# Another order and other PSUM banks ahead of the first MLP layer, and the first quarter of w_in in two loads

## The chip, the core and the metric

The kernel runs on one core of a Trainium2 chip. The metric is the device time of one execution in microseconds (us). Before the change the median of three runs is 305.06 us (304.82 to 306.04).

## What is computed

The reference is a sparse attention followed by a two-layer MLP. The attention has 8 batches of 8 heads, 576 positions and a head size of 64. Heads 0 to 3 look at the last 32 positions ("local"), heads 4 to 7 at all earlier positions with the same remainder mod 32 ("strided").

In short, with the softmax written as one function:

```python
scores = scale * np.matmul(q, k.transpose(0, 1, 3, 2))
mask_local = (rel >= 0) & (rel < stride)
mask_strided = (rel >= 0) & (pos[None, :] % stride == pos[:, None] % stride)
masks = np.stack([mask_local if h < H // 2 else mask_strided for h in range(H)], axis=0)
attn = softmax(np.where(masks, scores, -1e9))
x = (attn @ v).transpose(0, 2, 1, 3).reshape(4608, 512)
h = x @ w_in                                  # 512 -> 2048
g = np.where(h > 0.0, h, np.exp(np.minimum(h, 0.0)) - 1.0)
out = g @ w_out                               # 2048 -> 512
```

## The kernel before, in words

**Tiling.** The 4608 tokens go through the MLP in 9 chunks of 512. `xT` holds the attention output transposed: 128 partitions, 4 column blocks c, all tokens. Blocks c = 0 and 1 come from the local heads, c = 2 and 3 from the strided heads. `w_in` comes in four loads of 512 of its 2048 columns; each of its 16 column tiles m (128 wide) gives one PSUM tile h of layer 1, in four matmuls, one for each c. ELU is an Exp on ScalarE, a clamp and a max on VectorE, which writes `g`; layer 2 takes `g` and `w_out`.

The attention of a batch has four pairs of heads: `0s0` is batch 0, strided, first pair; `0s1` the second strided pair; `0l0` and `0l1` the local pairs. In batches 0 and 1 pair y of a kind fills one whole block of xT: `0l0` c = 0, `0l1` c = 1, `0s0` c = 2, `0s1` c = 3. Each pair is worked on in two halves u = 0 and 1.

**What sets the order.** The kernel runs under a manual schedule: `ORDER` (lines 35 to 145) is a list of tokens, and lines 702 to 704 issue them in that order. Each engine runs its own instructions strictly in that order; waits between engines follow from the data, from PSUM banks and from buffer pools. The eight PSUM banks are named in the tokens by hand. A matmul that writes a bank waits until whoever read that bank last is done. A token is a letter, then its arguments:

- `w.7.512.512`: filler matmuls on zeros (line 389), here two of 512 columns into bank 7; nobody reads them.
- `T.0s1.q.7`: transposes of q of pair 0s1 on TensorE into bank 7 (lines 403, 409, 412). The pair 0s0 goes in halves, from f32 data staged early. `c` copies a transpose out of PSUM on VectorE, `C` on ScalarE (lines 422 to 430).
- `S.0l1.1.23`: the scores of half u = 1 into banks 2 and 3 (line 455). `e`: Exp on ScalarE (462). `m`: the mask product on VectorE (469 strided, 475 local).
- `O.0l1.1.41`: the product with v, into bank 4, and the row sums, a product with ones, into bank 1 (482, 491 strided; 498, 503 local; function `pv`). `n`: Ln of the sums on ScalarE (553). `r`: Exp of minus that (558). `x`: the product on VectorE that writes xT (583).
- `V.0`: a VectorE copy of 32 rows of local v (587), which the local products with v need.
- `a.0.15.1`: layer 1 of chunk 0, tile m = 15, blocks c = 2 and 3, into bank 1. `b.0.15`: the same tile, blocks c = 0 and 1. `L`: all four blocks (function `l1`, line 610). `h`: the Exp of ELU (618). `i`, `j`: the clamp on VectorE or ScalarE; `g`: the max (636, 638). `Z`: layer 2 (644).
- `D`: a load, issued by GpSimd (POOL) (lines 233 to 280). `D.wi3.0` is the quarter of w_in with tiles 12 to 15; wi0, wi2 and wi1 follow. With one more argument, which no token of this ORDER uses, the quarter comes in two parts: .0 is the blocks c = 2 and 3, .1 the blocks 0 and 1 (lines 273 to 276). `F.mk` makes the local mask on POOL (348, 351) and `F.ml` lays it out on VectorE (356, 358).

Buffers that matter here: `e` has two, so the third Exp waits for the mask product of the first; `ln` has three, so an `n` waits for the `x` three before it; POOL has eight semaphores for loads, so a load is issued once the load eight before it has landed.

The stage that the change touches is all that stands ahead of layer 1: the attention of batch 0, some 22 us. Behind it the list of tokens stays as it is.

Of the kernel before, what the change touches and what calls it, by code (L numbers as in the profile page):

```python
# [33 lines left out]

ORDER = """
w.7.512.512.512.512.512.512.512.512 F.v1 D.kl.0.1 D.vs.0.0 F.vp D.ql.0.1 F.ms D.vs.0.1 T.0s0.q.0.7
D.kl.0.0 T.0s0.k.0.6 c.0s0.q.0 D.ql.0.0 c.0s0.k.0 w.0.512.512.172 T.0s0.k.1.7 S.0s0.0.01 C.0s0.k.1
T.0s0.q.1.6 e.0s0.0 D.vl.0 c.0s0.q.1 w.2.512.512.512 T.0s1.q.7 T.0s1.k.6 D.wi3.0 c.0s1.q S.0s0.1.01
C.0s1.k m.0s0.0 T.0l1.k.5 D.wi0.0 e.0s0.1 c.0l1.k w.2.403 S.0s1.1.67 S.0s1.0.23 e.0s1.1 m.0s0.1
w.4.512.406 T.0l1.q.5 e.0s1.0 m.0s1.1 D.wi2.0 O.0s0.1.47 c.0l1.q O.0s1.1.61 n.0s0.1 m.0s1.0 D.wi1.0  # L40
S.0l1.1.23 n.0s1.1 e.0l1.1 w.0.370 T.0l0.k.7 D.qs.1 O.0s0.0.51 r.0s1.1 O.0s1.0.03 F.mk r.0s0.1 T.0l0.q.2
x.0s1.1 C.0l0.k x.0s0.1 D.wo0.0 c.0l0.q n.0s1.0 w.5.224.224.224.224.206 S.0l1.0.67 n.0s0.0 F.ml
S.0l0.1.23 e.0l1.0 D.ks.1 r.0s1.0 w.4.512.512 S.0l0.0.67 m.0l1.1 r.0s0.0 m.0l1.0 x.0s1.0 e.0l0.0
w.4.512.512 V.0 e.0l0.1 O.0l1.1.41 x.0s0.0 n.0l1.1 O.0l1.0.07 m.0l0.0 D.wo1.0 n.0l1.0 O.0l0.0.32 m.0l0.1
r.0l1.1 O.0l0.1.75 r.0l1.0 x.0l1.1 x.0l1.0 n.0l0.0 a.0.15.1 n.0l0.1 a.0.14.6 r.0l0.0 a.0.12.4 r.0l0.1
a.0.13.5 D.wo2.0 x.0l0.0 x.0l0.1 D.wo3.0 b.0.15 b.0.14 h.0.15 b.0.12 h.0.14 i.0.15 b.0.13 a.0.0.0 h.0.12
b.0.0 a.0.1.2 b.0.1 i.0.14 g.0.15 h.0.0 a.0.3.7 D.vs.1 a.0.11.3 j.0.12 g.0.14 a.0.2.1 h.0.1 i.0.0 b.0.2
g.0.12 b.0.3 h.0.2 g.0.0 b.0.11 h.0.3 a.0.8.6 i.0.2 D.ql.1 h.0.11 i.0.1 a.0.6.4 g.0.2 h.0.13 a.0.5.0
b.0.8 g.0.1 a.0.4.1 D.kl.1 h.0.8 i.0.3 b.0.4 g.0.3 b.0.5 h.0.4 T.1s1.q.2 a.0.7.7 j.0.13 i.0.4 b.0.6
C.1s1.q g.0.4 b.0.7 D.vl.1 h.0.5 g.0.13 Z.0.1.0.2 h.0.6 i.0.5 Z.0.0.0.5 g.0.5 h.0.7 D.qs.2 j.0.6 i.0.8  # L50
a.0.9.1 i.0.7 a.0.10.0 g.0.8 b.0.9 g.0.6 j.0.11 b.0.10 g.0.7 h.0.9 T.1s1.k.6 Z.0.3.0.4 D.ks.2 h.0.10
g.0.11 j.0.10 Z.0.3.1.4 i.0.9 c.1s1.k g.0.10 Z.0.0.1.5 g.0.9 Z.0.1.1.2 D.kl.2 T.1s0.q.3 T.1s0.k.7
C.1s0.q Z.0.1.2.2 c.1s0.k S.1s0.1.01 S.1s1.0.67 Z.0.0.2.5 e.1s1.0 e.1s0.1 Z.0.0.3.5 m.1s0.1 m.1s1.0
S.1s1.1.01 S.1s0.0.67 e.1s1.1 Z.0.1.3.2 e.1s0.0 m.1s1.1 O.1s0.1.31 o.0.1 m.1s0.0 O.1s1.0.07 T.1l1.q.6
n.1s0.1 n.1s1.0 Z.0.3.2.4 c.1l1.q r.1s0.1 q.0.0 D.vs.2 r.1s1.0 O.1s1.1.76 x.1s1.0 T.1l1.k.5 n.1s1.1
O.1s0.0.21 c.1l1.k T.1l0.q.0 n.1s0.0 T.1l0.k.6 x.1s0.1 D.ql.2 Z.0.3.3.4 C.1l0.k c.1l0.q r.1s1.1 V.1
S.1l0.1.01 r.1s0.0 S.1l0.0.56 x.1s1.1 Z.0.2.0.3 e.1l0.0 q.0.3 X.qs.2 e.1l0.1 m.1l0.0 S.1l1.1.56 e.1l1.1
m.1l0.1 S.1l1.0.01 O.1l0.0.74 e.1l1.0 X.ks.2 m.1l1.1 O.1l0.1.65 x.1s0.0 Z.0.2.1.3 n.1l0.0 n.1l0.1
m.1l1.0 r.1l0.0 O.1l1.1.54 t.0.3 r.1l0.1 x.1l0.0 O.1l1.0.21 n.1l1.1 x.1l0.1 Z.0.2.2.3 n.1l1.0 r.1l1.1
t.0.0 r.1l1.0 Z.0.2.3.3 x.1l1.1 x.1l1.0 X.kl.2 W.2 L.1.12.7 L.1.1.6 h.1.12 i.1.12 L.1.6.5 h.1.1 g.1.12  # L60
o.0.2 D.qs.3 L.1.0.4 i.1.1 h.1.6 g.1.1 L.1.4.7 h.1.0 i.1.6 g.1.6 L.1.5.6 X.ql.2 h.1.4 D.ks.3 i.1.0 j.1.4
L.1.3.5 g.1.0 D.vs.3 h.1.5 t.0.1 g.1.4 L.1.2.4 D.vl.2 h.1.3 i.1.5 i.1.3 h.1.2 g.1.3 L.1.10.7 S.2s1.0.01
S.2s1.1.23 e.2s1.0 g.1.5 D.ql.3 e.2s1.1 L.1.15.5 i.1.2 h.1.10 g.1.2 L.1.7.6 h.1.15 m.2s1.1 i.1.15
S.2s0.0.01 S.2s0.1.23 h.1.7 X.qs.3 g.1.15 L.1.13.4 e.2s0.1 i.1.10 j.1.7 L.1.9.5 m.2s0.1 g.1.10 L.1.8.3
g.1.7 h.1.9 e.2s0.0 i.1.9 L.1.14.7 X.ks.3 h.1.13 g.1.9 L.1.11.6 h.1.8 i.1.13 h.1.14 i.1.8 Z.1.2.0.5
# [83 lines left out]
def kernel(  # L149
# [455 lines left out]
    def l1(ch, m, cs, bk=None):  # L605
        ch, m = int(ch), int(m)
        if bk is not None:
            tiles["h", ch, m] = ps[:, int(bk), :]
        for c in cs:
            nc.tensor.matmul(  # L610
                tiles["h", ch, m], lhsT=w_in_sb[:, c, m * 128:(m + 1) * 128],
                rhs=xT[:, c, ch * CHUNK:(ch + 1) * CHUNK],
                start=(c == 2), stop=(c == 1), skip_group_check=True)
# [121 lines left out]
```

## Time and profile before

| | |
|---|---|
| median of three runs | 305.06 us |
| lowest and highest run | 304.82 and 306.04 us |
| the profiled execution's own time | 305.3 us |
| its span, first to last instruction | 303.6 us |
| ScalarE (ACT) busy | 222.9 us (73%) |
| VectorE (DVE) busy | 224.4 us (74%) |
| loads by POOL (queue q0) | 19.47 MB |

The profile has one such execution. PE is the matmul side of TensorE, PEld its weight loads. In a timeline the first column is the start in us, the second the time until the group's last instruction ends; `x8` is how many instructions are in the group, and a bracket says how long the engine sat idle before it and what ended that. Matmuls overlap: the time from one start to the next counts, not their duration. Ends of matmuls are modelled. A table by stretches gives the busy time of each engine in each stretch, with the number of instructions in brackets.

### The profile page before, as it was taken

The page shows a single profiled execution, that of the slowest core. Times are in us where ns is not written, and L with a number is a line of the kernel's source. Part 1 is how long each engine was busy: PE and PEld are TensorE (multiplying, and loading weights), DVE is VectorE, ACT ScalarE, POOL GpSimd, SP SyncE. Part 2 cuts the span into 40 slices and gives each one's busy share as a digit, 9 for nine tenths or more (in the row PEclk, how much of TensorE's full clock was granted, in tenths as well). Part 3 has the DMA queues.
Part 4 walks back from the last instruction along what each step waited for, and adds up shares of the span by engine and source line. Part 5 has one row for each costly group of instructions (what it writes and reads, how often), then busy time and mean ns, then how long its engine had stood idle before and what let it go on. Part 6 is the DMA issues. An engine that isn't in the chain of part 4 may idle for free.

```text
span 303.6 us, 6241 instructions
## 1 busy us (share of the span) xinstructions
PE 297.1 (98%) x2331; PEld 147.5 (49%) x2331; DVE 224.4 (74%) x440; ACT 222.9 (73%) x402; POOL 81.5 (27%) x111
## 2 busy tenths in 40 slices
...
GB/s 165 187 206 206 207 194 166 168 223 146 128 143 152 191 193 138 160 143 164 140 188 208 73 173 163 129 38 36 38 69 0 37 35 0 37 36 0 37 138 104
DMA packets 107357, 37.62 MB, mean 124 GB/s; under 512 B 89152, under 2 KB 102848, under 8 KB 107328
## 3 DMA queue, kind: packets, MB, share of 16 engines
q0 software_dynamic: 69728, 19.47, 63.6%
...
## 4 chain that ended last, share of the span: by engine, by line
PE 89%; ACT 5%; DVE 3%; issue 1%; DVEq 0%; ACTq 0%
PE ps L610 38%; PE ps L644 38%; PE ps L455 3%; PE ps L389 2%; PE ps L518 2%; PE ps L525 2%; ACT e L462 1%; ACT ln L558 1%; ACT ln L553 1%; PE ps L674 1%; DVE g L638 1%; DVE he L627 1%; PE ps L412 1%; PE ps L403 1%; PE ps L409 1%
## 5 line engine op out<-in xcount | busy, mean ns | idle before, releaser
L644 PE MATMUL ps<-w_out_sb,g 128*128 128x512 bf16 x560 | 133.4, 379 | 0.0
L610 PE MATMUL ps<-xT,w_in_sb 128*128 128x512 bf16 x576 | 131.2, 379 | 0.8 <-DVE xT L583 0.4
L618 ACT ACTIVATE he<-ps 128x512 f32<-128x512 f32 x144 | 80.2, 596 | 25.8 <-PE ps L610 24.8
L610 PEld LDWEIGHTS <-w_in_sb 128*128 128x128 bf16 x576 | 54.9, 98 | 65.3 <-issue 1.9
L644 PEld LDWEIGHTS <-g 128*128 128x128 bf16 x560 | 50.8, 98 | 54.2
L638 DVE TENSOR_TENSOR g<-he,ps 128x512 bf16<-128x512 bf16 x103 | 68.3, 681 | 1.6
L583 DVE TENSOR_TENSOR xT<-ps,ln 64x576 bf16<-64x576 f32 (+1 forms) x64 | 42.6, 678 | 22.8 <-ACT ln L558 21.2
L627 DVE TENSOR_SCALAR he<-he 128x512 bf16<-128x512 f32 x103 | 44.0, 440 | 12.5 <-ACT he L618 11.8
L462 ACT ACTIVATE e<-ps 72x576 bf16<-72x576 f32 (+1 forms) x64 | 38.7, 647 | 9.9 <-PE ps L455 7.8
L553 ACT ACTIVATE ln<-ps 64x576 f32<-64x576 f32 (+1 forms) x64 | 36.4, 584 | 9.2 <-PE ps L518 5.1
L558 ACT ACTIVATE ln<-ln 64x576 f32<-64x576 f32 (+1 forms) x64 | 38.4, 621 | 1.2
L636 DVE SCALAR_TENSOR_TENSOR g<-he,ps 128x512 bf16<-128x512 bf16 x41 | 27.4, 679 | 4.9 <-ACT he L625 4.7
L625 ACT ACTIVATE he<-he 128x512 bf16<-128x512 f32 x41 | 25.4, 630 | 1.8 <-DVE g L638 1.1
...
L650 ACT COPY osb<-ps 128x512 f32<-128x512 f32 x17 | 9.9, 584 | 17.3 <-PE ps L644 10.6
L650 DVE COPY osb<-ps 128x512 f32<-128x512 f32 x18 | 12.2, 684 | 13.5 <-PE ps L644 13.4
...
L475 DVE TENSOR_TENSOR pm<-e,mask_l 128x576 bf16<-128x576 bf16 x32 | 14.2, 454 | 7.4 <-ACT e L462 6.5
L469 DVE TENSOR_TENSOR pm<-e,mask_s 72x576 bf16<-72x576 bf16 x32 | 14.2, 448 | 3.7 <-ACT e L462 3.3
L233 POOL DMA_DIRECT2D vs<-in_v_dram x8 | 5.3, 658 | 32.0 <-DVE vsp L590 31.0
L233 POOL DMA_DIRECT2D ks<-in_k_dram x7 | 4.8, 685 | 27.6 <-DMA kTs<-ks 25.8
L518 PEld LDWEIGHTS <-vsp 72*128 72x128 bf16 x192 | 9.3, 98 | 5.5 <-DVE pm L469 0.5
...
## 6 DMA issues: line engine op xcount, KB each, us to landing
...
```

The costliest lines, as they stand in the source:

```text
L462: nc.scalar.activation(e[0:R], tiles.pop(("S", key, u))[0:R], ACT.Exp, scale=scale)
L553: nc.scalar.activation(t, s_ps, ACT.Ln)
L558: nc.scalar.activation(t, t, ACT.Exp, scale=-1.0)
L583: nc.vector.tensor_mul(dst, o_ps, rc)
L610: nc.tensor.matmul(tiles["h", ch, m], lhsT=w_in_sb[:, c, m * 128:(m + 1) * 128], rhs=xT[:, c, ch * CHUNK:(ch + 1) * CHUNK], start=(c == 2) ...
L618: nc.scalar.activation(e, tiles["h", i[0], i[1]], ACT.Exp)
L625: nc.scalar.activation(e1, e, ACT.Relu, bias=1.0, scale=-1.0)
L627: eng.tensor_scalar(e1, e, scalar1=1.0, scalar2=1.0, op0=ALU.min, op1=ALU.subtract)
L636: nc.vector.scalar_tensor_tensor(dst, e1, -1.0, h, op0=ALU.mult, op1=ALU.max)
L638: nc.vector.tensor_tensor(dst, e1, h, op=ALU.max)
L644: nc.tensor.matmul(ops, lhsT=g[ch % 2][:, m, kk * 128:(kk + 1) * 128], rhs=w_out_sb[:, m, :], start=(m == 0), stop=(m == MC - 1), skip_gro ...
L650: eng(o_sb, tiles.pop(("o", int(ch), int(kk))))
```

## The change

The tokens ahead of layer 1 stand in another order, with other banks; three new things are in the code.

1. **Fillers.** `w.0` loses one of 512 columns, and `w.2` (three of 512, then one of 403) is gone. Behind them five groups with 4438 columns become four groups, of two or three fillers of 512, with 5120 columns. Seven fewer filler matmuls in all.
2. **Second pair at once.** `T.0s1.q` and `T.0s1.k` follow `T.0s0.q.1` directly, into banks 3 and 4.
3. **Pair 0's products first.** `O.0s0.0` and `O.0s0.1`, with their `n`, `r`, `x`, come ahead of those of 0s1; before, three of the four came the other way round. `m.0s1.0` now stands ahead of `c.0l1.q`, `n.0s1.1` ahead of `e.0l1.1`; all four strided `r` come ahead of `e.0l1.0`; all four strided `x` and `F.ml` come ahead of `m.0l1.0` and `V.0`.
4. **Masks early.** `F.mk` goes from behind `D.qs.1` to behind the first w_in quarter on POOL, and `F.ml` moves up on VectorE.
5. **w_in's first quarter in two loads,** `D.wi3.0.0` (blocks 2 and 3) and `D.wi3.0.1`.
6. **Layer 1.** `a.0.15.1` moves between the products of 0l1 and those of 0l0. Blocks 1 and 0 are taken in that order everywhere (`b`, `L`), and for the tiles 15, 14, 12 of chunk 0 block 1 of all three (`p`) comes ahead of block 0 (`P`).

```diff
-D.kl.0.0 T.0s0.k.0.6 c.0s0.q.0 D.ql.0.0 c.0s0.k.0 w.0.512.512.172 T.0s0.k.1.7 S.0s0.0.01 C.0s0.k.1
-T.0s0.q.1.6 e.0s0.0 D.vl.0 c.0s0.q.1 w.2.512.512.512 T.0s1.q.7 T.0s1.k.6 D.wi3.0 c.0s1.q S.0s0.1.01
-C.0s1.k m.0s0.0 T.0l1.k.5 D.wi0.0 e.0s0.1 c.0l1.k w.2.403 S.0s1.1.67 S.0s1.0.23 e.0s1.1 m.0s0.1
-w.4.512.406 T.0l1.q.5 e.0s1.0 m.0s1.1 D.wi2.0 O.0s0.1.47 c.0l1.q O.0s1.1.61 n.0s0.1 m.0s1.0 D.wi1.0
-S.0l1.1.23 n.0s1.1 e.0l1.1 w.0.370 T.0l0.k.7 D.qs.1 O.0s0.0.51 r.0s1.1 O.0s1.0.03 F.mk r.0s0.1 T.0l0.q.2
-x.0s1.1 C.0l0.k x.0s0.1 D.wo0.0 c.0l0.q n.0s1.0 w.5.224.224.224.224.206 S.0l1.0.67 n.0s0.0 F.ml
-S.0l0.1.23 e.0l1.0 D.ks.1 r.0s1.0 w.4.512.512 S.0l0.0.67 m.0l1.1 r.0s0.0 m.0l1.0 x.0s1.0 e.0l0.0
-w.4.512.512 V.0 e.0l0.1 O.0l1.1.41 x.0s0.0 n.0l1.1 O.0l1.0.07 m.0l0.0 D.wo1.0 n.0l1.0 O.0l0.0.32 m.0l0.1
-r.0l1.1 O.0l0.1.75 r.0l1.0 x.0l1.1 x.0l1.0 n.0l0.0 a.0.15.1 n.0l0.1 a.0.14.6 r.0l0.0 a.0.12.4 r.0l0.1
-a.0.13.5 D.wo2.0 x.0l0.0 x.0l0.1 D.wo3.0 b.0.15 b.0.14 h.0.15 b.0.12 h.0.14 i.0.15 b.0.13 a.0.0.0 h.0.12
+D.kl.0.0 T.0s0.k.0.6 c.0s0.q.0 D.ql.0.0 c.0s0.k.0 w.0.512.172 T.0s0.k.1.7 S.0s0.0.01 C.0s0.k.1
+T.0s0.q.1.6 e.0s0.0 D.vl.0 c.0s0.q.1 T.0s1.q.3 T.0s1.k.4 D.wi3.0.0 c.0s1.q S.0s0.1.01 C.0s1.k m.0s0.0
+T.0l1.k.5 D.wi3.0.1 e.0s0.1 c.0l1.k S.0s1.1.67 S.0s1.0.23 e.0s1.1 m.0s0.1 w.4.512.512 e.0s1.0 m.0s1.1
+F.mk O.0s0.0.40 D.wi0.0 D.wi2.0 O.0s0.1.51 n.0s0.0 T.0l1.q.6 n.0s0.1 m.0s1.0 r.0s0.0 c.0l1.q w.7.512.512
+r.0s0.1 F.ml S.0l1.1.23 O.0s1.1.70 D.wi1.0 x.0s0.0 n.0s1.1 x.0s0.1 O.0s1.0.61 e.0l1.1 T.0l0.k.4 n.0s1.0
+T.0l0.q.5 m.0l1.1 D.qs.1 r.0s1.1 c.0l0.q r.0s1.0 x.0s1.1 C.0l0.k S.0l1.0.01 x.0s1.0 w.2.512.512.512
+e.0l1.0 S.0l0.0.45 S.0l0.1.23 D.wo0.0 m.0l1.0 V.0 e.0l0.0 D.ks.1 m.0l0.0 w.7.512.512.512 e.0l0.1
+O.0l1.1.41 n.0l1.1 O.0l1.0.56 m.0l0.1 a.0.15.1 D.wo1.0 n.0l1.0 O.0l0.0.07 r.0l1.1 O.0l0.1.23 r.0l1.0
+x.0l1.1 x.0l1.0 n.0l0.0 n.0l0.1 a.0.14.6 r.0l0.0 a.0.12.4 r.0l0.1 a.0.13.5 p.0.15 p.0.14 p.0.12 D.wo2.0
+x.0l0.0 x.0l0.1 D.wo3.0 P.0.15 P.0.14 h.0.15 P.0.12 h.0.14 i.0.15 b.0.13 a.0.0.0 h.0.12 b.0.0 a.0.1.2
...
-                start=(c == 2), stop=(c == 1), skip_group_check=True)
+                start=(c == 2), stop=(c == 0), skip_group_check=True)
...
-        "a": lambda ch, m, bk: l1(ch, m, (2, 3), bk), "b": lambda ch, m: l1(ch, m, (0, 1)),
-        "L": lambda ch, m, bk: l1(ch, m, (2, 3, 0, 1), bk), "h": exp_h,
+        "a": lambda ch, m, bk: l1(ch, m, (2, 3), bk), "b": lambda ch, m: l1(ch, m, (1, 0)),
+        "p": lambda ch, m: l1(ch, m, (1,)), "P": lambda ch, m: l1(ch, m, (0,)),
+        "L": lambda ch, m, bk: l1(ch, m, (2, 3, 1, 0), bk), "h": exp_h,
```

The tokens behind `h.0.12` are the same in both kernels.

More of the change, by code (lines that the diff above doesn't have):

```diff
@@ L47 @@
[L47 to L61, printed above, removed]
@@ L62 @@
-L.1.3.5 g.1.0 D.vs.3 h.1.5 t.0.1 g.1.4 L.1.2.4 D.vl.2 h.1.3 i.1.5 i.1.3 h.1.2 g.1.3 L.1.10.7 S.2s1.0.01
+D.kl.0.0 T.0s0.k.0.6 c.0s0.q.0 D.ql.0.0 c.0s0.k.0 w.0.512.172 T.0s0.k.1.7 S.0s0.0.01 C.0s0.k.1
+T.0s0.q.1.6 e.0s0.0 D.vl.0 c.0s0.q.1 T.0s1.q.3 T.0s1.k.4 D.wi3.0.0 c.0s1.q S.0s0.1.01 C.0s1.k m.0s0.0
+T.0l1.k.5 D.wi3.0.1 e.0s0.1 c.0l1.k S.0s1.1.67 S.0s1.0.23 e.0s1.1 m.0s0.1 w.4.512.512 e.0s1.0 m.0s1.1
+F.mk O.0s0.0.40 D.wi0.0 D.wi2.0 O.0s0.1.51 n.0s0.0 T.0l1.q.6 n.0s0.1 m.0s1.0 r.0s0.0 c.0l1.q w.7.512.512
@@ new lines @@
+x.0l0.0 x.0l0.1 D.wo3.0 P.0.15 P.0.14 h.0.15 P.0.12 h.0.14 i.0.15 b.0.13 a.0.0.0 h.0.12 b.0.0 a.0.1.2
+b.0.1 i.0.14 g.0.15 h.0.0 a.0.3.7 D.vs.1 a.0.11.3 j.0.12 g.0.14 a.0.2.1 h.0.1 i.0.0 b.0.2 g.0.12 b.0.3
+h.0.2 g.0.0 b.0.11 h.0.3 a.0.8.6 i.0.2 D.ql.1 h.0.11 i.0.1 a.0.6.4 g.0.2 h.0.13 a.0.5.0 b.0.8 g.0.1
+a.0.4.1 D.kl.1 h.0.8 i.0.3 b.0.4 g.0.3 b.0.5 h.0.4 T.1s1.q.2 a.0.7.7 j.0.13 i.0.4 b.0.6 C.1s1.q g.0.4
+b.0.7 D.vl.1 h.0.5 g.0.13 Z.0.1.0.2 h.0.6 i.0.5 Z.0.0.0.5 g.0.5 h.0.7 D.qs.2 j.0.6 i.0.8 a.0.9.1 i.0.7
@@ new lines @@
+a.0.10.0 g.0.8 b.0.9 g.0.6 j.0.11 b.0.10 g.0.7 h.0.9 T.1s1.k.6 Z.0.3.0.4 D.ks.2 h.0.10 g.0.11 j.0.10
+Z.0.3.1.4 i.0.9 c.1s1.k g.0.10 Z.0.0.1.5 g.0.9 Z.0.1.1.2 D.kl.2 T.1s0.q.3 T.1s0.k.7 C.1s0.q Z.0.1.2.2
+c.1s0.k S.1s0.1.01 S.1s1.0.67 Z.0.0.2.5 e.1s1.0 e.1s0.1 Z.0.0.3.5 m.1s0.1 m.1s1.0 S.1s1.1.01 S.1s0.0.67
+e.1s1.1 Z.0.1.3.2 e.1s0.0 m.1s1.1 O.1s0.1.31 o.0.1 m.1s0.0 O.1s1.0.07 T.1l1.q.6 n.1s0.1 n.1s1.0
+Z.0.3.2.4 c.1l1.q r.1s0.1 q.0.0 D.vs.2 r.1s1.0 O.1s1.1.76 x.1s1.0 T.1l1.k.5 n.1s1.1 O.1s0.0.21 c.1l1.k
```

7 lines of the change are left out of this document (added).

## The prediction

> **What bounds the kernel now.** I read the page's busy times, then the table by stretches, then the chain of waits ahead of layer 1, then each engine's timeline there.
>
> ```profile
> span 303.6 us, 6241 instructions
> PE 297.1 (98%) x2331; PEld 147.5 (49%) x2331; DVE 224.4 (74%) x440; ACT 222.9 (73%) x402; POOL 81.5 (27%) x111
> 22.00:30.00 8.00, 8.00 (x45) 3.78 (x44) 6.54 (x14) 5.64 (x12) 2.08 (x4) 1.00 1.24 206
> 100.00:200.00 100.00, 99.98 (x795) 49.00 (x793) 83.27 (x154) 87.69 (x153) 33.95 (x41) 1.00 1.24 157
> ```
>
> The first two numbers of a stretch row are its length and PE's busy time: behind the 22nd microsecond PE is never let go for long. So the kernel's time is the moment at which layer 1 runs, plus a fixed amount of matmul work. What the change moves lies ahead of that. I therefore ask one thing: when does PE reach `b.0.13`, the first matmul behind the rewritten tokens that is the same in both? What it gains there it should keep to the end.
>
> ```profile
> 15.27 0.61 PE L389 MATMUL ps<-zero 128*128 128x512 bf16 x2
> 15.80 0.31 PE L498 MATMUL ps<-pm,ones 128*64 128x288 bf16 x2
> 16.48 0.23 PE L503 MATMUL ps<-pm,vl 128*64 128x96 bf16 x1 [0.36 <-DVE vl L587]
> 16.88 0.32 PE L503 MATMUL ps<-pm,vl 128*64 128x96 bf16 x5 [0.17 <-issue]
> 16.99 0.32 PE L498 MATMUL ps<-pm,ones 128*64 128x288 bf16 x2
> 17.70 0.31 PE L498 MATMUL ps<-pm,ones 128*64 128x288 bf16 x2
> 18.07 1.90 PE L610 MATMUL ps<-xT,w_in_sb 128*128 128x512 bf16 x8
> 20.33 9.23 PE L610 MATMUL ps<-xT,w_in_sb 128*128 128x512 bf16 x42 [0.35 <-DVE xT L583]
> ```
>
> The row at 20.33 starts the six matmuls of `b.0.15`, `b.0.14`, `b.0.12`. The row at 18.07 has eight matmuls; 42 in a row take 9.23 us, so one every 0.216 us. Hence `b.0.13` starts at 20.33 + 6 x 0.216 = **21.62 us**. Two stalls stand ahead of it: PE waits for the copy of v (VectorE L587), until 16.48, and for the last product into xT (L583), until 20.33. Between the first and second matmul at L503 lies a hole of 0.40 us (16.48 to 16.88) in which the profile shows no wait; I can't explain it and keep it.
>
> **The change, part by part.** I carry each engine's order forward with the spacings of its rows.
>
> *Opening.*
>
> ```profile
> 4.64 1.17 PE L403 MATMUL ps<-identity_f,g 72*128 72x72 f32 x8
> 5.61 1.20 PE L389 MATMUL ps<-zero 128*128 128x512 bf16 x3
> 6.60 0.46 PE L403 MATMUL ps<-identity_f,g 72*128 72x72 f32 x4
> 6.99 0.33 PE L455 MATMUL ps<-qTs,kTs 64*72 64x72 bf16 x8
> 7.55 0.81 PE L389 MATMUL ps<-zero 128*128 128x512 bf16 x3
> 8.20 0.42 PE L409 MATMUL ps<-identity,qs 72*128 72x72 bf16 x8
> 8.82 0.33 PE L455 MATMUL ps<-qTs,kTs 64*72 64x72 bf16 x8
> ```
>
> The copy and the Exp that follow, on VectorE and ScalarE:
>
> ```profile
> 7.75 0.46 DVE L422 CAST qTs<-ps 128x288 bf16<-128x288 f32 x1 [1.45 <-PE ps L403]
> 9.46 1.97 ACT L462 ACTIVATE e<-ps 72x576 bf16<-72x576 f32 x3
> ```
>
> Three 512-column fillers take 0.65 us at 7.55 (to 8.20). The three at 5.61 have 1196 columns and take 0.99: TensorE is still at half pace there (eight transposes at 4.64 take 0.97, four at 6.60 with the change of array shape behind them 0.39). Dropping one filler of `w.0` brings the transposes at 6.60 forward by 0.43, but they then run at half pace (0.48 and 0.1 for the change of shape, against 0.39): net 0.24, scores at 6.75. Dropping `w.2` lets the transposes of 0s1 start at 7.27 and not 8.20. The next scores (8.82) then wait for VectorE's copy of the second q half, which was 7.75 to 8.21 and comes 0.24 earlier, to 7.97: they start at 8.02, **0.8 us earlier**. The three Exp in the row at 9.46 follow them and the mask products in the same rhythm; the third, `e.0s1.0`, ended at 11.43 (9.46 + 1.97), so it started 0.65 before that, at 10.78, and now starts near 9.99.
>
> [...]
>
> *Most of that is given back.* VectorE now runs `m.0s1.0` ahead of `c.0l1.q`. `e.0s1.0` ends at 10.63, the mask product takes 10.66 to 11.11, the copy 11.03 to 11.48, so the scores `S.0l1.1` start at 11.53; before:
>
> ```profile
> 11.64 0.30 PE L455 MATMUL ps<-qTl,kTl 64*128 64x96 bf16 x6
> 11.99 0.65 ACT L462 ACTIVATE e<-ps 128x576 bf16<-128x576 f32 x1
> 12.53 0.77 ACT L558 ACTIVATE ln<-ln 128x288 f32<-128x288 f32 x2
> 13.20 0.63 ACT L430 COPY kTl<-ps 128x576 bf16<-128x576 bf16 x1
> 13.72 0.72 ACT L553 ACTIVATE ln<-ps 128x288 f32<-128x288 f32 x2
> 14.31 0.67 ACT L462 ACTIVATE e<-ps 128x576 bf16<-128x576 f32 x1
> ```
>
> From start to start ScalarE needs 0.54 for an `e`, 0.67 for two `r`, 0.52 for the copy `C`, 0.59 for two `n`. In the new order `n.0s1.1` comes first. It waits for the sums of `O.0s1.1`, which stands behind `S.0l1.1` on PE (11.76), so it starts at 12.10. Then run without a gap `n`, `e.0l1.1`, `n`, two `r`, `C`: 0.30 + 0.54 + 0.30 + 0.67 + 0.52 brings `e.0l1.0` to 14.43, against 14.31. Its mask product starts at 15.11, against 15.01: here the new order is **0.1 us late**.
>
> *VectorE then gains.*
>
> ```profile
> 14.51 0.96 DVE L475 TENSOR_TENSOR pm<-e,mask_l 128x576 bf16<-128x576 bf16 x2
> 15.39 0.45 DVE L583 TENSOR_TENSOR xT<-ps,ln 128x288 bf16<-128x288 f32 x1
> 15.87 0.55 DVE L587 COPY vl<-vl 32x1472 bf16<-32x1472 bf16 x1
> ...
> 18.13 0.82 DVE L583 TENSOR_TENSOR xT<-ps,ln 128x288 bf16<-128x288 f32 x2 [0.48 <-ACT ln L558]
> 19.45 0.82 DVE L583 TENSOR_TENSOR xT<-ps,ln 128x288 bf16<-128x288 f32 x2 [0.50 <-ACT ln L558]
> ```
>
> Before, an `x` (15.39) stood between the mask product at 15.01 and the copy of v. It is now done earlier. The copy starts 0.38 behind the mask product (15.01 to 15.39), at 15.49 to 15.59, and ends by 16.1. The matmuls on v start near **16.15 and not 16.48**.
>
> *PE from there.* Now I sum: to the sums of `O.0l1.0` 0.51 as before, hole included (16.48 to 16.99); that product 0.37 with the change of array shape behind it (17.70 to 18.07); `a.0.15` 0.43; change of shape 0.1; `O.0l0.0` and `O.0l0.1` 0.27 + 0.37 (the first without a change of shape); then six matmuls of `a` and six of `p` and `P`, 12 x 0.216 = 2.59. Together 4.64, so `b.0.13` starts at **20.8**, against 21.62. This holds if nothing waits. `p` needs only block 1, whose `x` end 0.3 us earlier than before (18.95): reached at 19.5, free. `P` is reached at 20.1 and needs the last `x`, before at 20.27 by the row at 19.45; its chain starts with the sums of `O.0l1.0`, 0.33 us earlier, so it ends near 19.95. That is a margin of 0.15. The stall of 20.33 goes; late next is PE itself.
>
> *w_in in two loads, masks early.*
>
> ```profile
> 8.20 3.00 POOL L275 DMA_DIRECT2D w_in_sb<-in_moe_w_in_dram  x4
> ...
> 14.39 0.74 POOL L279 DMA_DIRECT2D w_out_sb<-in_moe_w_out_dram  x1 [0.48 <-DMA vl<-in_v_dram]
> 17.81 0.74 POOL L279 DMA_DIRECT2D w_out_sb<-in_moe_w_out_dram  x1 [2.68 <-DMA w_in_sb<-in_moe_w_in_dram]
> 20.35 0.74 POOL L279 DMA_DIRECT2D w_out_sb<-in_moe_w_out_dram  x1 [1.80 <-DMA w_in_sb<-in_moe_w_in_dram]
> 22.98 0.65 POOL L233 DMA_DIRECT2D g<-in_v_dram  x1 [1.89 <-DMA w_in_sb<-in_moe_w_in_dram]
> 25.44 0.64 POOL L233 DMA_DIRECT2D xT<-in_q_dram  x1 [1.81 <-DMA w_in_sb<-in_moe_w_in_dram]
> ```
>
> Each issue from 14.39 on was released by a landing: local v by 14.39, the four quarters of w_in by 17.81, 20.35, 22.98, 25.44. The loads land one behind the other, some 2.55 us a quarter. Half a quarter should land 1.27 behind v or 1.27 ahead of the whole: 15.7 to 16.5. `a.0.15` now wants it at 17.0, `p` wants the rest at 19.5 (17.81). So the split is what lets `a.0.15` stand there; it gains nothing else. POOL's extra issue (under 0.8) and `F.mk` ahead of the second quarter delay the later issues by up to 1.4 us. What hides that is the backlog: the four quarters were issued within 3.00 us from 8.20, and the last landed at 25. If that cover were gone, PE would reach the third quarter (`a.0.11`, the 19th matmul from 20.33, at 24.2 before and 23.4 now) 0.9 us too soon and the gain would vanish. With the cover the margin there is 0.4 (22.98 against 23.4), so a gain over 1.2 us would be cut off there.
>
> *p ahead of P.* The first Exp of ELU waits for four matmuls and not two, so ScalarE's work starts 0.4 us earlier, not 0.8. It still starts earlier than before, so nothing waits longer for it in absolute time; I cost it at nothing, at most the 0.43. Blocks in the order 1, 0 in later chunks change which product into xT is needed third; with no wait of PE there in the trace it costs nothing, at most 0.22 once, in chunk 1.
>
> Sum: 0.8 us. On the profiled execution 305.3 becomes 304.5; on the median, 0.2 below it, 305.06 becomes **304.3**.
>
> **The rivals.** *The hole goes (304.0).* If the 0.40 us hole does not come back, PE gains at most 0.3 more, since `a.0.15` then waits for `n.0l1.1` to leave bank 1. For it: no wait explains the hole. Against: the same products are issued. Spread of the runs (304.82 to 306.04) takes a third of this case past 303.5.
>
> *The half lands late (305.0).* If the first half of w_in lands with the whole, at 17.8, `a.0.15` blocks PE, and both products of 0l0 with it: 17.85 + 0.43 + 0.1 + 0.64 + 2.59 = 21.6, no gain. For it: loads are in flight for many microseconds, so the order inside the backlog is not seen. Against: the landings above come in strict order. [...]
>
> *The clock falls back (306.9).* There are fewer fillers early, and by the walk above PE waits some 0.4 us for the copy near 11 (its fillers end near 10.9). If TensorE drops to half pace as layer 1 starts and needs as long as from the start of its work to full pace (1.26 to 6.6, the fillers at 1.26 and 7.55), 5.3 us at 0.43 per matmul are 12.4 matmuls, each 0.21 late: 2.6 us, 304.3 + 2.6. It decides once PE's busy share falls below what the old order has. Against: the lowest there is this, and the columns of filler behind 10 us rise from 4438 to 5120.
>
> ```profile
> 16.00:18.00 2.00, 1.47 (x32) 1.17 (x30) 1.61 (x4) 1.67 (x6) 0.19 (x1) 1.00 1.24 206
> 1.26 3.59 PE L389 MATMUL ps<-zero 128*128 128x512 bf16 x8 [1.26 <-DVE zero L304]
> ```
>
> **How the numbers follow.** Forecast 304.3: chance 0.55. Hole gone 0.15. Half late 0.15. Clock 0.15. About 0.5% (1.5 us) is what a measurement of this kernel can tell from no change: faster 0.05, same 0.80, slower 0.15. The range leaves out the clock case and the far end of the first rival: 303.5 to 305.9, the upper end being no gain with the spread of the runs above the median.
>
> **What would show it.** Right: `S.0s0.1` near 8.0, `S.0l1.1` near 11.5, the matmuls on v near 16.15, no wait for xT at `P`, `b.0.13` at 20.8, and from there a constant lead. Wrong: a wait for w_in at `a.0.15`; 512-column matmuls 0.43 apart behind 7 us; a wait for weights near 23; or a lead at `b.0.13` that is lost before the end.

## The result and the profile after

The changed kernel takes 306.03 us in the median of 22 runs (305.02 to 309.17), the kernel before 305.44 us in 22 runs on the same chip: a ratio of 1.0028, with a 95% interval from 1.0016 to 1.004. That is 0.6 us slower, where 0.8 us faster was forecast; it stays within 0.5%. The ratios here and below compare the fast runs and are not quotients of the medians; four executions of 312 to 1077 us (three of before beside e1 to e4, one of e4) are left out of them. The profiled execution took 305.94 us, with a span of 304.2.

The page of the changed kernel shows where to look: a row of the 40 slices, each 7.6 us, gives the granted clock (the share of its full clock that TensorE was given) in tenths.

```profile
span 304.2 us, 6184 instructions
PE 294.0 (97%) x2285; PEld 146.8 (48%) x2324; DVE 224.3 (74%) x440; ACT 223.2 (73%) x402; POOL 81.0 (27%) x112
PEclk9979999999999999999999999999999999999999
```

The third slice has a 7 where the kernel before has full clock. The timeline of PE there, after:

```profile
6.57 0.33 PE L455 MATMUL ps<-qTs,kTs 64*72 64x72 bf16 x8
7.94 0.33 PE L455 MATMUL ps<-qTs,kTs 64*72 64x72 bf16 x8
11.47 0.30 PE L455 MATMUL ps<-qTl,kTl 64*128 64x96 bf16 x6 [0.22 <-DVE qTl L426]
12.69 0.45 PE L412 MATMUL ps<-identity,ql 72*64 72x72 bf16 x16
14.55 0.30 PE L455 MATMUL ps<-qTl,kTl 64*128 64x96 bf16 x6 [1.41 <-ACT kTl L430]
15.96 1.46 PE L389 MATMUL ps<-zero 128*128 128x512 bf16 x3
17.59 0.45 PE L503 MATMUL ps<-pm,vl 128*64 128x96 bf16 x6
18.46 0.95 PE L610 MATMUL ps<-xT,w_in_sb 128*128 128x512 bf16 x2
19.96 4.28 PE L610 MATMUL ps<-xT,w_in_sb 128*128 128x512 bf16 x18
```

Up to 12.69 this is the forecast's walk. Then PE stands still for 1.41 us, for a copy by ScalarE. Behind that, three fillers at 15.96 take 1.46 us, some 0.4 from one to the next and not 0.22: TensorE runs at half pace. The table by stretches gives the clock (the third number from the end), which was 1.00 in all four stretches before:

```profile
14.00:16.00 2.00, 1.29 (x21) 0.69 (x23) 1.01 (x3) 1.27 (x3) 0.74 (x2) 0.94 1.32 202
16.00:18.00 2.00, 2.00 (x15) 0.83 (x15) 1.50 (x4) 1.23 (x3) 1.15 (x3) 0.50 1.26 209
18.00:20.00 2.00, 2.00 (x29) 0.98 (x26) 0.82 (x2) 1.64 (x6) 0.58 (x1) 0.70 1.25 210
20.00:22.00 2.00, 1.95 (x11) 0.94 (x11) 0.82 (x2) 1.06 (x4) 0.74 (x1) 1.00 1.23 202
```

So `b.0.13` starts near 22.56 us, not at 20.8; 21.62 before. (Aligned matmul by matmul from the end, it is 0.94 late.) Of this, 0.78 us is left at the end. (The granted clock does not show every half pace: it stands at 1.00 in the opening too, where fillers come 0.43 apart.) ScalarE's rows there, after:

```profile
12.05 0.41 ACT L553 ACTIVATE ln<-ps 128x288 f32<-128x288 f32 x1 [0.24 <-PE ps L482]
12.36 0.64 ACT L462 ACTIVATE e<-ps 128x576 bf16<-128x576 f32 x1
12.89 0.42 ACT L553 ACTIVATE ln<-ps 128x288 f32<-128x288 f32 x1
13.18 0.79 ACT L558 ACTIVATE ln<-ln 128x288 f32<-128x288 f32 x2
13.85 0.65 ACT L430 COPY kTl<-ps 128x576 bf16<-128x576 bf16 x1
14.90 0.65 ACT L462 ACTIVATE e<-ps 128x576 bf16<-128x576 f32 x1 [0.40 <-PE ps L455]
```

The copy `C.0l0.k` (13.85) now stands behind both pairs of `n` and `r`, and `S.0l1.0` behind the copy. The scores are those of pair 0l1, the copy is of pair 0l0: both lie in one tile, and the first window of the scores reaches 32 columns into the part that the copy writes. (The mask hides these columns, so the scores do not need the copy.)

### The profile page after: what moved, and what is told of

It is laid out like the page before. It is cut to its first block, busy times and chain, and to the rows that moved or that the text cites. A ratio compares the mean times of both kernels' runs of the same rounds, so it can differ in the third digit from the quotient of the medians.

```text
span 304.2 us, 6184 instructions
## 1 busy us (share of the span) xinstructions
PE 294.0 (97%) x2285; PEld 146.8 (48%) x2324; DVE 224.3 (74%) x440; ACT 223.2 (73%) x402; POOL 81.0 (27%) x112
## 4 chain that ended last, share of the span: by engine, by line
PE 92%; ACT 2%; issue 2%; DVE 2%; DMA 2%; ACTq 0%
PE ps L610 40%; PE ps L644 39%; PE ps L455 4%; PE ps L518 2%; PE ps L525 2%; DMA g<-in_k_dram 2%; PE ps L674 1%; ACT e L462 1%; PE ps L389 1%; PE ps L498 1%; PE ps L409 1%; PE ps L412 0%; ACT ln L558 0%; PE ps L503 0%; PE ps L482 0%
## 5 line engine op out<-in xcount | busy, mean ns | idle before, releaser
L644 PE MATMUL ps<-w_out_sb,g 128*128 128x512 bf16 x541 | 130.7, 379 | 1.3 <-issue 0.6
L627 DVE TENSOR_SCALAR he<-he 128x512 bf16<-128x512 f32 x103 | 43.8, 439 | 12.2 <-ACT he L618 11.4
L650 ACT COPY osb<-ps 128x512 f32<-128x512 f32 x17 | 9.9, 584 | 17.3 <-PE ps L644 10.6
L243 POOL DMA_DIRECT2D ql<-in_q_dram x24 | 19.9, 836 | 5.2 <-DMA qs<-in_q_dram 2.7
```

The lines of the kernel that those rows point to most:

```text
L644: nc.tensor.matmul(ops, lhsT=g[ch % 2][:, m, kk * 128:(kk + 1) * 128], rhs=w_out_sb[:, m, :], start=(m == 0), stop=(m == MC - 1), skip_gro ...
L650: eng(o_sb, tiles.pop(("o", int(ch), int(kk))))
```

## The experiments

In each table row below, the last three columns say how much later (negative: earlier, a lead) the same matmul starts than in the first profile of before, counted back from the last matmul: at `b.0.13` (in e8 without the eight matmuls that it leaves out behind it), at 76 us and at the end. Each kernel has one profile; the medians are of 7 to 12 runs (22 in the first row), beside the kernel before on the same chip. No ratio is as much as 0.5% from 1.

| kernel | median, before (us) | ratio (95%) | b.0.13 | 76 us | end |
|---|---|---|---|---|---|
| after | 306.03, 305.44 | 1.0028 (1.0016 to 1.004) | +0.94 | +1.06 | +0.78 |
| e1 scores first | 305.22, 305.57 | 0.9994 (0.9981 to 1.0008) | -0.71 | -0.12 | +0.26 |
| e2 fillers in the wait | 305.19, 305.57 | 0.9998 (0.9983 to 1.0013) | -0.23 | +0.55 | +0.49 |
| e3 before, fewer fillers | 305.94, 305.57 | 1.0021 (1.0006 to 1.0036) | +0.10 | +0.21 | +0.14 |
| e4 before, p and P | 305.60, 305.57 | 1.0003 (0.999 to 1.0016) | -0.82 | -0.53 | +0.06 |
| e5 = e1, one load | 305.40, 305.30 | 1.0012 (0.9993 to 1.0032) | -0.55 | -0.23 | +0.12 |
| e6 before again | 305.35, 305.30 | 0.9997 (0.9988 to 1.0006) | +0.05 | +0.12 | +0.25 |
| e7 before, 1.73 more | 306.50, 305.30 | 1.0036 (1.0022 to 1.005) | +0.82 | +1.08 | +1.19 |
| e8 before, 1.73 less | 305.15, 305.30 | 0.9992 (0.998 to 1.0003) | -0.35 | -0.42 | -0.71 |
| e9 = e1, scores of 2s later | 306.22, 305.33 | 1.0037 (1.0015 to 1.006) | -1.16 | +0.34 | +0.37 |
| e10 before, the same | 305.70, 305.33 | 1.0014 (1.0002 to 1.0025) | -0.63 | -0.01 | +0.48 |
| e11 = e1, Exp of 2s1 later | 305.46, 305.23 | 1.0014 (0.9995 to 1.0033) | -1.22 | -0.01 | -0.23 |
| e12 before, the same | 305.30, 305.23 | 1.0 (0.9989 to 1.0011) | -0.17 | +0.17 | +0.27 |
| e13 = e1, v load early | 304.90, 305.21 | 0.9989 (0.9979 to 1.0) | -0.76 | +1.27 | +1.47 |
| e14 before, the same | 305.33, 305.21 | 1.0006 (0.9992 to 1.0019) | -0.49 | -0.16 | -0.20 |

**The wait and the clock (e1, e2, e3).** Theory: the copy ahead of the scores makes the hole, and the hole drops the clock. Rivals: the clock falls by itself, or for other work.

```diff
 e1 (on after)
-C.0l0.k S.0l1.0.01 x.0s1.0
+S.0l1.0.01 C.0l0.k x.0s1.0
 e2 (on after)
-C.0l0.k S.0l1.0.01 x.0s1.0 w.2.512.512.512
+C.0l0.k w.2.512.512.512.512.512.512 S.0l1.0.01 x.0s1.0
 e3 (on before)
-w.5.224.224.224.224.206 S.0l1.0.67
+S.0l1.0.67
-w.4.512.512 S.0l0.0.67
+S.0l0.0.67
-w.4.512.512 V.0
+V.0
```

> The changed kernel with one token moved: the scores S.0l1.0 now stand ahead of the copy C.0l0.k in the list, so they no longer take the 32 columns of kT that this copy writes (those columns are masked either way). Theory A (the copy is what holds these scores, the 1.41 us hole on PE that follows lets the clock fall, and both together ate the forecast gain): the scores start near 13.4 and not 14.55, no hole over 0.5 us on PE, no 512-column matmul 0.43 apart behind 7 us, granted clock 1.00, b.0.13 near 20.9 and not 22.56, time 0.6 to 0.9 us below the kernel before. Rival B (the scores wait for bank 0 or 1, held by the Ln of 0s1): they stay at 14.5, nothing changes. Rival C (the clock falls because fewer fillers stand early, not because of this hole): scores at 13.4, but the clock stays at 0.994 and the time within 0.3 us of before.

> The changed kernel with six fillers of 512 columns ahead of S.0l1.0 in place of the three behind it: PE has work during the wait, which itself stays. Theory A (hole lets the clock fall; the wait costs by itself too): granted clock 1.00 in all executions, S.0l1.0 still at 14.5, matmuls 0.216 apart from 7 us on, b.0.13 near 21.5 to 21.8, time 0.6 to 0.8 us below the changed kernel, within 0.3 us of the kernel before. Rival C (the clock falls because of fewer fillers early): clock 0.994, no gain. Rival D (the clock is a matter of chance between executions, whatever PE does): clock as often below 1 as in the changed kernel, two in three.

> The kernel before without its nine fillers between 13.3 and 15.9 us (3150 columns); its order, banks and loads stay. Theory A (PE's idle share ahead of layer 1 decides over the clock): granted clock below 1, matmuls 0.43 apart for about 3 us near layer 1, time 0.7 to 2 us above the kernel before. Rival D (chance, or something else in the changed kernel): clock 1.00 and time within 0.3 us of before, as nobody reads the fillers.

PE in e1, then in e2:

```profile
13.35 0.21 PE L455 MATMUL ps<-qTl,kTl 64*128 64x96 bf16 x1
13.83 0.29 PE L455 MATMUL ps<-qTl,kTl 64*128 64x96 bf16 x5 [0.27 <-ACT ln L553]
14.05 0.82 PE L389 MATMUL ps<-zero 128*128 128x512 bf16 x3
18.31 4.06 PE L610 MATMUL ps<-xT,w_in_sb 128*128 128x512 bf16 x18
```

```profile
13.43 1.46 PE L389 MATMUL ps<-zero 128*128 128x512 bf16 x6
14.92 0.56 PE L455 MATMUL ps<-qTl,kTl 64*128 64x96 bf16 x18
18.79 3.41 PE L610 MATMUL ps<-xT,w_in_sb 128*128 128x512 bf16 x15
```

In e1 the hole is gone, three fillers take 0.82 us, and `b.0.13` comes at 18.31 + 12 x 0.216 = 20.90, almost as forecast. In e2 the scores still wait until 14.92 for the copy, but fillers run meanwhile: the clock stays at 1.00 and `b.0.13` comes at 21.38. So the hole, not the lateness, costs the clock. e3 makes waits of 0.49, 0.49 and 0.90 us in the old order, the first for the same copy, and gets the same clock:

```profile
13.45 0.66 PE L455 MATMUL ps<-qTl,kTl 64*128 64x96 bf16 x12 [0.49 <-ACT kTl L430]
14.59 0.30 PE L455 MATMUL ps<-qTl,kTl 64*128 64x96 bf16 x6 [0.49 <-ACT e L462]
16.04 0.45 PE L503 MATMUL ps<-pm,vl 128*64 128x96 bf16 x6 [0.90 <-DVE vl L587]
```

```profile
14.00:16.00 2.00, 0.65 (x14) 0.26 (x7) 1.95 (x7) 2.00 (x6) 0.57 (x1) 1.00 1.28 206
16.00:18.00 2.00, 1.96 (x31) 1.57 (x31) 1.65 (x5) 1.82 (x6) 0.74 (x2) 0.50 1.24 207
```

It is not chance alone: the mean clock is 0.998 or more in all 12 runs of e1 and all 12 of e2, and 0.994 or less in all 10 of e3 and in 15 of the 22 of the changed kernel. In the time, e2 is back at the kernel before. Two expected sizes were missed: e1 is 0.35 us below before in the median and not 0.6 to 0.9, and e3 0.4 us above (0.6 by the ratio) and not 0.7 to 2.

**What the other parts do alone (e4, e5).** e4 is the old order with blocks 1, 0 and `p` ahead of `P`; e5 is e1 with `D.wi3.0.0` and `D.wi3.0.1` made one `D.wi3.0` again.

```diff
 e4 (on before)
-b.0.15 b.0.14 h.0.15 b.0.12
+p.0.15 p.0.14 p.0.12 ... P.0.15 P.0.14 h.0.15 P.0.12
```

> The kernel before with one part of the change alone: blocks in the order 1, 0, and p ahead of P for the tiles 15, 14, 12 of chunk 0. My step (PE has work during the wait for the last product into xT, 0.53 us from the end of the eight matmuls of a to 20.33): p runs from 19.80 to 20.45, b.0.13 starts at 21.1 and not 21.62, time 0.4 to 0.5 us below before. Rival (the later first Exp of ELU or the later block 1 in chunk 1 gives it back): b.0.13 early, but the lead is gone by 60 us and the time within 0.2 us of before.

> The kernel with the scores of 0l1 ahead of the copy of k, and besides it the first quarter of w_in in one load again. If the split is what lets a.0.15 stand ahead of the products of 0l0, a.0.15 waits for the whole quarter, which landed at 17.6 us after the change, and O.0l0.0 and all behind it come some 0.5 us later: b.0.13 near 21.2 instead of 20.9 to 20.7, and a wait of about 0.6 us for w_in in the row of the first L610 matmuls. If the quarter lands in time anyway (rival: the two loads only split a landing that is early enough), b.0.13 stays within 0.1 us. In both cases the whole time moves by no more than 0.3 us, because a lead of this size was lost behind layer 1 in two runs.

In e4 the wait of 0.35 us for xT is gone, and `b.0.13` is 0.82 early. Of this, 0.30 is there already when `a.0.15` starts (17.77, not 18.07). The wait itself was a rare one: it makes `b.0.15` 0.53 late in the first profile of before, but only 0.13 in five others of the same order (e6, e8, e10, e12, e14). So `p` is worth some 0.13 us, too little for a median to show. In e5 `a.0.15` waits for the load, as the row shows, but only for 0.21 us, and `b.0.13` comes 0.16 later than in e1:

```profile
17.31 0.60 PE L610 MATMUL ps<-xT,w_in_sb 128*128 128x512 bf16 x2 [0.21 <-DMA w_in_sb<-in_moe_w_in_dram]
```

Neither is faster than before at the end. In their profiles e1 and e4 have all or most of the forecast lead at `b.0.13` and none of it at the end, and their medians do not show it (e1's interval still reaches 0.6 us faster). So a second step of the forecast is in doubt; e7 and e8 test it.

**Lead and lag (e6, e7, e8).** Theory: what comes early at layer 1 is held up later; what comes late stays late. Rival: the steps behind 22 us are chance. e7 has `w.1` with eight fillers of 512 ahead of `a.0.15`; e8 leaves out blocks 2 and 3 of the tiles 4, 7, 9 and 10 of chunk 0.

> The kernel before once more, with nothing changed: how far do two executions of one program differ, and where? If the steps seen behind 30 us in the other runs (about +0.2 near 61 and 65 us, up to -0.4 near 92, +0.3 near 139, +0.1 near 210) are chance between executions, some of them appear here against the first profile too. If they come from what the kernels do ahead of layer 1, this profile agrees with the first within 0.1 us all along. The median agrees with that of before within 0.2 us.

> The kernel before with eight fillers of 512 columns ahead of a.0.15: 1.73 us of work more on PE just ahead of layer 1. Theory: what PE is late behind the 22nd microsecond has little slack, so 1.4 to 1.8 us of it reach the end (median near 307.1). Rival: later waits for transfers swallow half a microsecond or more of a lag too, and the end moves by 1.2 us or less.

> The kernel before without blocks 2 and 3 of the tiles 4, 7, 9 and 10 of chunk 0, that is eight matmuls of layer 1 left out between about 26 and 31 us: 1.73 us of PE's work less, early, with all loads of w_in landed. Theory: transfers that arrive at fixed times hold PE again later, near 61 us above all, so that less than half of it reaches the end, 0.8 us or less (median 304.8 or higher). Rival: PE is the bound all along and what was seen behind 30 us is chance; then 1.5 to 1.8 us reach the end (median near 303.9).

e7 came 0.82 late to `b.0.13` (its opening ran 0.4 us early, and 0.5 went into the wait for xT) and 1.19 late to the end; its ratio is 0.36% up, about 1.1 us. That is the rival's range (1.2 or less) and not the 1.4 to 1.8 expected; 0.5 of the 1.73 never reached `b.0.13`. In e8 1.73 us of PE's work are gone, and the median moves by 0.15 us; the interval ends at 0.6 us faster. So most of a lag passes and most of a lead does not. In e8 one sees it being lost: most of it at 30 to 34 us, to ScalarE and VectorE (2.07 us early at 29 us, 0.88 at 35), then 0.36 near 65:

```profile
30.13 1.89 PE L645 MATMUL ps<-w_out_sb,g 128*128 128x512 bf16 x8 [0.45 <-ACT qTs L426]
33.20 0.42 PE L409 MATMUL ps<-identity,xT 72*128 72x72 bf16 x8 [0.31 <-DVE g L639]
65.00 3.61 PE L611 MATMUL ps<-xT,w_in_sb 128*128 128x512 bf16 x16 [0.48 <-DVE g L639]
```

What holds it at 30 to 34 us no run tested; the next runs take up the smaller loss near 65. e6 shows that chance has a share: the unchanged kernel has steps of +0.11 (65 us), -0.22 (92 us) and +0.27 (139 us) against its own first profile.

**What holds a lead near 65 us (e9 to e14).** First theory: the scores of batch 2 (`S.2s1`) wait for k, which a transposing DMA brings near 61 us, and the ELU queues behind their Exp. e9 and e10 move these scores, and those of `2s0`, one tile of layer 1 later, and `h.1.10` ahead of `e.2s1.0` (the diff shows the first part); e11 and e12 only put `h.1.10` ahead of `e.2s1.0`.

```diff
 e9 on e1, e10 on before
-L.1.10.7 S.2s1.0.01 S.2s1.1.23 e.2s1.0 g.1.5 D.ql.3 e.2s1.1 L.1.15.5 i.1.2 h.1.10
+L.1.10.7 g.1.5 D.ql.3 L.1.15.5 S.2s1.0.01 S.2s1.1.23 i.1.2 h.1.10 e.2s1.0
 e11 on e1, e12 on before
-S.2s1.1.23 e.2s1.0 g.1.5
+S.2s1.1.23 h.1.10 e.2s1.0 g.1.5
```

> The kernel with the scores of 0l1 ahead of the copy of k, and besides it the scores of batch 2's first strided pairs (2s1, 2s0) each one tile of layer 1 later on PE, and h.1.10 ahead of e.2s1.0 on ScalarE. Theory: the transposed k of batch 2 lands near 61 us in every kernel, and the scores that wait for it, then the Exp behind them, hold ScalarE, VectorE and so PE: that is where a lead is lost. Then there is no wait of PE and none of ScalarE for these scores, the wait for g near 65 us shrinks to under 0.2, the lead of 0.55 at 59 us is still over 0.4 at 70 us, and the median falls by 0.3 to 0.6 us below that of before. Rival: VectorE's slow clamps beside the issues of loads set the time near 65 us; then the wait for g stays at 0.4, and the median stays within 0.25 us of before.

> The kernel before with that second edit alone: scores of 2s1 and 2s0 one tile of layer 1 later, h.1.10 ahead of e.2s1.0. Before, PE does not wait for the transposed k, ScalarE does for these scores, and PE then 0.2 to 0.3 us for g. Theory: the wait for g goes, so the end comes 0.1 to 0.3 us earlier. Rival (VectorE is the bound there): no change beyond 0.1 us.

> The kernel with the scores of 0l1 ahead of the copy of k, and besides it only h.1.10 ahead of e.2s1.0 on ScalarE; the scores stay where they were. Theory: near 62 us ScalarE idles some 0.7 us for the scores of 2s1, which wait for the transposed k, and the ELU of tiles 10 and 15 queues behind the two Exp; with h.1.10 in that idle time, h.1.15 ends some 0.3 us earlier, the wait of PE for g near 65 us falls from 0.40 to 0.1 or less, and the lead at 70 us is larger by 0.2 to 0.3. The median then lies 0.2 to 0.6 us below that of before. Rival: the mask product, which stands ahead of the next clamp on VectorE, comes later by as much as the Exp; then the wait for g stays at 0.3 or more and the median does not move.

> The kernel before with h.1.10 ahead of e.2s1.0 alone. Theory: the wait for g near 65 us (0.3 in the first profile) falls to 0.1 or less, and the median falls by 0.1 to 0.3 us. Rival: as for the other, no change beyond 0.1 us. Against it the other kernel also shows what the earlier arrival at layer 1 is worth once this wait is gone: 0.3 us or more by the theory, nothing by the rival.

All four missed: the wait of PE for g near 65 us stayed, 0.95 in e9, 0.61 in e10, 0.41 in e11 and e12, and none is faster; the intervals of e9 and e10 lie above 1. In e10 the clamp took its usual 0.43, so something else makes the wait there, perhaps the moved scores. But e11 showed what holds PE in the others. VectorE in e1 and in e11 (the clamp of tile 15, L627), and GpSimd in the same two:

```profile
63.83 0.70 DVE L627 TENSOR_SCALAR he<-he 128x512 bf16<-128x512 f32 x1 [0.51 <-ACT he L618]
65.17 0.42 DVE L627 TENSOR_SCALAR he<-he 128x512 bf16<-128x512 f32 x1
```

```profile
63.47 1.17 DVE L627 TENSOR_SCALAR he<-he 128x512 bf16<-128x512 f32 x1
```

```profile
61.82 0.65 POOL L233 DMA_DIRECT2D ks<-in_k_dram  x1 [4.70 <-DMA kTs<-ks]
63.09 1.18 POOL L260 DMA_DIRECT2D vl<-in_v_dram  x1
```

```profile
61.92 0.66 POOL L233 DMA_DIRECT2D ks<-in_k_dram  x1 [4.99 <-DMA kTs<-ks]
63.20 1.19 POOL L260 DMA_DIRECT2D vl<-in_v_dram  x1
```

The clamp starts 0.36 earlier in e11 and ends later: it takes 0.70 and 1.17 us instead of the next one's 0.42, and ends at 64.53 and 64.64, both times 0.26 behind the end of the issue at L260 (64.27 and 64.39). In e2, e5, e6, e8, e9 and e12 it ends 0.26 behind it too. Behind 20 us in the 16 profiles, 147 clamps take over 0.43 us; each overlaps an issue and ends 0.22 to 0.26 us behind one's end, while none of the 1,206 clamps without an issue beside them takes over 0.43. All 147 start 0.25 us or more into an issue. But some two dozen that start as far into one, most of them issues of other loads, are not held. By what an issue holds a clamp, and why not always, no run shows.

So theory two: GpSimd issues that load when the transposed k has landed, and holds the clamp, which holds g and PE. The earlier Exp of e11 did bring the clamp forward; the hold swallowed that. e13 and e14 give the load's issue an earlier place.

```diff
 e13 on e1, e14 on before
-D.ks.3
+D.vl.2 D.ks.3
-L.1.2.4 D.vl.2 h.1.3
+L.1.2.4 h.1.3
```

> The kernel with the scores of 0l1 ahead of the copy of k, and besides it the load of batch 2's local v one place earlier in GpSimd's queue, ahead of the strided k of batch 3: its two issues (1.18 and 0.74 us) then come near 57 us instead of 63, the strided k and v follow the landing near 61, and the short issues of q come 1.9 us earlier. Theory (a clamp that meets an issue of GpSimd is held until 0.26 us behind that issue's end): the clamp near 63.8 takes 0.42 instead of 0.70, the wait for g near 65 falls from 0.40 to 0.15 or less, and the lead at 76 us is 0.3 larger than in the kernel without this edit, unless a clamp near 57 to 59 is held instead. Rival (VectorE's sheer amount of work, or the late Exp, sets that point): the wait stays at 0.35 to 0.45. In the median 0.1 to 0.4 us less than before by the theory, no difference by the rival; a later landing of k of batch 3 would show as a new wait near 85 us.

> The kernel before with that earlier place of the local v load alone. Theory: the clamp of tile 15 near 64 us takes 0.42, the wait for g near 65 us is 0.2 or less, and the median moves by no more than 0.2 us. Rival: the wait stays at 0.25 to 0.4, as in the other profiles of this order. The difference to the other kernel is again what the earlier arrival at layer 1 is worth: 0.3 us or more if the held clamps were what swallowed it, nothing if it is lost at later places all the same.

The clamp takes 0.43 in both, and the profile marks no wait of PE near 65 us in either. VectorE and PE in e14:

```profile
64.06 0.43 DVE L627 TENSOR_SCALAR he<-he 128x512 bf16<-128x512 f32 x1 [0.39 <-ACT he L618]
```

```profile
63.73 0.43 PE L455 MATMUL ps<-qTs,kTs 64*128 64x72 bf16 x16
64.10 4.78 PE L610 MATMUL ps<-xT,w_in_sb 128*128 128x512 bf16 x20
```

No gap over 0.15 us is left in these twenty, where e8 waits 0.48. Counted from start to start, the matmul at 65.26 still comes 0.29 late in e14, as in e13, against 0.56 to 0.66 in e1, e2, e5, e8, e11 and e12, whose clamp takes 0.70 us or more. So a held clamp costs PE some 0.3 us here. The move is not the only way to escape it: in before, e4 and e7 the clamp happened to miss the hold, with the issue in its old place, and the delay is 0.29 too. The medians: e13 0.31 us below that of before, e14 0.12 above, so the early arrival at layer 1 now seems worth some 0.4 us; this is not shown, as the two intervals overlap. e13 is the fastest kernel of this study, faster than the changed one; against before its interval just touches 1. Its profiled execution is its slowest bar none (306.66 us): PE waited for w_out at 41 us, ahead of the moved issue and so not because of it, and later another clamp was held beside the moved issue, which is the hazard of such an order (PE, then VectorE and GpSimd of e13):

```profile
41.24 1.02 PE L644 MATMUL ps<-w_out_sb,g 128*128 128x512 bf16 x4 [0.92 <-DMA w_out_sb<-in_moe_w_out_dram]
```

```profile
59.04 1.07 DVE L627 TENSOR_SCALAR he<-he 128x512 bf16<-128x512 f32 x1
```

```profile
58.65 1.22 POOL L260 DMA_DIRECT2D vl<-in_v_dram  x1
```

What is left open: how much of a lead is lost at each place in the mean of many executions. The steps at 34 us (in e1, e4, e11, e14) and 139 us go with held clamps at 30.2 to 31.0 and near 135 us in the same profiles (0.66 us at 135.0 in before, 1.03 at 134.9 in e6), but no run moved those issues, so for them the cause is argued and not shown. The largest step at 34 us, that of e8, goes without one: its clamp at 30.73 takes 0.42.

## Why the prediction was wrong, step by step

Two steps failed: the walk to `e.0l1.0`, which left out a wait and with it the clock, and the step from `b.0.13` to the end.

- **Opening: right, but the gain is smaller.** Scores at 6.57 and 7.94 (6.75 and 8.02 forecast). Over all profiles the second scores start from 7.90 to 8.32 in the new opening and from 8.20 to 9.04 in the old one, on average at 8.10 and 8.58: 0.5 earlier and not 0.8. The profile of before (8.82) was one of the later ones. At `b.0.13` it is the same: the five kernels with the scores first (e1, e5, e9, e11, e13) lie 0.88 ahead of that profile on average, but six profiles of the old order (before, e6, e8, e10, e12, e14) lie 0.27 ahead of it too. The new order is worth some 0.6 there.
- **"Most of that is given back": its first half was right** (scores 11.47, `n.0s1.1` 12.05; that `n` stands ahead of `e.0l1.1` in the old list too, but waits now for a product behind these scores), **its end failed.** `e.0l1.0` came at 14.90 and not at 14.43, "0.1 us late" became 0.6. The walk followed ScalarE alone, and took `S.0l1.0` for done when the Exp was free. The scores waited for `C.0l0.k`, and came at 14.55 against 13.35 to 13.83 where they stand first (e1). The old order has the same dependency, 13.90 against the copy of 13.20 to 13.83, hidden there by five fillers; e3, which leaves these out, shows it as a wait.
- **The clock, the rival with 0.15, happened.** Its point was named (PE's busy share below the old order's), but the search looked at a wait of 0.4 us near 11 us and not at the 1.41 us behind 13. Its price was mis-sized: half pace lasted 3.41 us and not 5.3, and lay ahead of layer 1, from 15.78 to 19.19 us, where PE otherwise waits part of the time. So it cost `b.0.13` 1.18 us (22.56 against 21.38 in e2; 1.55 counted from the scores at 14.55 and 14.92), not 2.6. In 15 of the 22 runs after, the mean clock is 0.994 or lower (median 306.27); in 7 it is 0.998 or more (median 305.57, no better than before).
- **"VectorE then gains" and the sum of 4.64: the end is right in e1, by luck.** There `b.0.13` came at 20.90, against 20.8. But the matmuls on v came at 16.65 and not 16.15 (0.5 late), and from there PE took 4.25 us and not 4.64 (the hole of 0.40 us at L503 that the sum kept did not come). The two errors cancel. e11, which opened earlier, has 16.13 and 20.40.

```profile
16.65 0.32 PE L503 MATMUL ps<-pm,vl 128*64 128x96 bf16 x6 [0.20 <-DVE vl L587]
```

- **w_in in two loads: right in kind.** In GpSimd's timeline after, an issue is released by the first half of w_in at 16.56 us; without the split `a.0.15` waited 0.21 us (e5), less than the 0.6 expected of e5, because the whole quarter landed by 17.3. *The half lands late* falls.

```profile
16.56 0.75 POOL L279 DMA_DIRECT2D w_out_sb<-in_moe_w_out_dram  x1 [0.32 <-DMA w_in_sb<-in_moe_w_in_dram]
```

- **p ahead of P: right in kind.** The wait for xT is gone in every kernel with it, but it made `b.0.15` 0.53 late in one profile of the old order alone, and 0.13 in five others.
- ***The hole goes*: the hole of 0.40 us does not come back**, in the unchanged kernel either (e6). In the old order PE waits 0.28 there for the mask product, and less for xT, so `b.0.13` comes 4.75 us behind the first matmul on v and not 5.14; in the new order it comes 4.25 behind it and not 4.64. So the hole belonged to that one record and drops out of the difference. In e6:

```profile
16.92 0.32 PE L503 MATMUL ps<-pm,vl 128*64 128x96 bf16 x6 [0.36 <-DVE vl L587]
17.77 0.31 PE L498 MATMUL ps<-pm,ones 128*64 128x288 bf16 x2 [0.28 <-DVE pm L475]
```

- **"What it gains there it should keep to the end": failed,** and kept the time near 305 even without the copy's wait and the clock (e1, 305.22). A PE that is busy for 99.98 of 100 us was read as a PE that sets the time. It has little slack for being late (e7: 0.82 at `b.0.13`, 1.19 at the end), but its inputs come from other engines and from transfers, and at 30 to 34 and near 65 us PE waits for them when it is early (e8: 0.45, 0.31 and 0.48 us). A lead over 1.2 us was expected to be cut off at the third quarter of w_in. e9's lead of 1.16 was cut there to 0.67, e11's of 1.22 was not, so the landing moves between executions. In e9:

```profile
23.53 0.82 PE L610 MATMUL ps<-xT,w_in_sb 128*128 128x512 bf16 x3 [0.32 <-DMA w_in_sb<-in_moe_w_in_dram]
```
